# A second DMA transpose in place of seven TensorE transposes, with GpSimd taking two heads of a subtraction

## The chip, the cores and the metric

The kernel runs on one core of a Trainium2 chip. The metric is device time in microseconds (us). A core has five engines that run their own instruction queues side by side and wait for each other by semaphores: TensorE (PE in the profile; weight loads are listed apart as PEld), VectorE (DVE), ScalarE (ACT), GpSimd (POOL) and SyncE (SP), which here only issues transfers. Transfers run on 16 DMA engines that all queues share.

## The reference

Linear attention, followed by a two-layer network without biases:

```
q_s = exp(q - max(q, axis=-1));  q_s = q_s / sum(q_s, axis=-1)      # softmax over the 64 features
k_s = exp(k - max(k, axis=2));   k_s = k_s / sum(k_s, axis=2)       # softmax over the 576 positions
kv  = einsum('bhsd,bhse->bhde', k_s, v)                             # 64 x 64 for each batch and head
att = einsum('bhsd,bhde->bhse', q_s, kv)
x   = att transposed to (batch * position, head * feature)          # 4608 x 512
out = maximum(0.01 * h, h) @ w_out   with  h = x @ w_in             # 512 -> 2048 -> 512
```

q, k and v are 8 batches x 8 heads x 576 positions x 64 features of float32; the output is 4608 x 512 float32.

## The kernel before

**Two jobs, one instruction stream.** The network works on nine tiles of 512 tokens (`t` from 0 to 8). For a tile, `layer1` (L548, its matmul is L550) makes 16 blocks of 128 x 512 in PSUM, ScalarE puts each through the leaky ReLU into `gj` (L559), and `layer2` (L570, matmul L571) sums them into the output; then the result is copied to `out_sb` (L565) and stored (L568). The attention of the batches 1 to 7 is woven into these tiles. The call `at(t, u, f, ...)` hangs pieces of work on a place, and `run(t, u)` emits them there: u from 0 to 15 is after layer 1's block u, u from 16 to 31 is within layer 2. Tile 0 is cut finer: u from 0 to 31 are the blocks of its two halves and 32 to 47 are the 16 steps of layer 2 (so `at(0, 44, ...)` comes after its thirteenth step). The schedule is written out by hand: on each engine, instructions stand in the order in which the code emits them, and an instruction that waits holds up all that is behind it on its engine.

**Layout.** A batch's q, k or v is 128 partitions x 4 heads of the partition's half x 9 rows x 64 features (`HL`, `R`, `D`; one partition half holds four of the eight heads, the other half the other four). "Heads 0, 1" (`H0`) and "heads 2, 3" (`H1`) are the halves of the `HL` axis, and `gg` 0 and 1 are the same halves in the cross products. `R7` is rows 0 to 6, `RE` rows 7 and 8.

**k of a batch.** `k_tree` takes the maximum over the nine rows by four `tensor_tensor` steps (L153), `k_allmax` (L155) takes it over the partitions into `kall`, `k_sub` subtracts it in place (L186), `k_exp` makes `ke` (L194, ScalarE). `v_cast` makes the bfloat16 v with a column of ones (L204 on ScalarE, L206 on GpSimd). `kv` multiplies `ke` and v on TensorE (L328); `kd_make` divides by the sum (L348, L349).

**q of a batch.** `q_max` (L229), `q_sub` (L291), `q_exp` (L299), `q_sum` with the reciprocal (L308, L310), `q_norm` (L315). Then q has to be turned, so that features lie on partitions. Either TensorE does it against an identity matrix, and the result is copied from PSUM (`q_turn_first` L268 with `q_keep_first` L281, L282, L284, L286; `q_transpose` L432 with `q_keep` L447), or SP issues a DMA transpose (`q_turn` L538, `turn_next` L544). `cross` (L464) multiplies the turned q by `kd`.

**Batch 1** is special. Its rows 0 to 6 are wanted in tile 1, together with batch 0's last row: `attend_next` (L525) makes these cross products near the end of tile 0, heads 0, 1 first and then heads 2, 3, and copies them to `xT` (L533). Before the change, heads 0, 1 are turned by a DMA transpose of seven blocks into the tile `X1`, issued by `next_loads` ahead of four loads, and heads 2, 3 by seven TensorE transposes into `qT`, copied from PSUM half by ScalarE and half by VectorE. Rows 7 and 8 go by a later DMA transpose of four blocks into the end of `X1`. The exponential of heads 0, 1 stands before that of heads 2, 3 everywhere.

**Queues around the change.** SP's queue holds, in order: batch 1's k and q, `more_loads` (batch 1's v in two halves, batch 2's first k half), `next_loads`, the stores of tile 0, the loads of batch 3. GpSimd's holds the loads of the weights (L126, L131), then batch 1's `q_sub` of heads 0, 1, the `k_sub` of head 0, the `q_sub` of heads 2, 3.

Of the kernel before, what the change touches and what calls it, by code (L numbers as in the profile page):

```python
# [25 lines left out]
def kernel(  # L26
# [48 lines left out]
    def load(src, b, name, cuts, t=None):  # L75
        t = raw(name) if t is None else t
        flat = src[b].rearrange("h s d -> (h s d)").rearrange(
            "(hl p r d) -> p hl r d", hl=HL, p=P, r=R
        )
        for hs, rs in cuts:  # L80
            nc.sync.dma_start(  # L81
                out=t[:, hs, rs].rearrange("p h r d -> p h (r d)"),
                in_=flat[:, hs, rs].rearrange("p h r d -> p h (r d)"),
            )
        return t
# [133 lines left out]
    def q_begin(b):  # L219
        st[b]["qe"] = qe_pool.tile([P, R, HL, D], BF16, name="qe")  # L220
        if b == 1:
            st[b]["X1"] = const_pool.tile([P, R7.stop + 2 * (R - R7.stop), P], BF16, name="X1")
        if b < 2:
            st[b]["qT"] = qT_pool.tile([P, NB, R, L], BF16, name="qT", tag="qT")

    def q_max(b, rs, hs=ALLH):
# [50 lines left out]

    def q_keep_first(eng, b, gg, rs=RA):
        o, i = st[b]["qT"][:, gg::2, rs], st[b]["ps2", gg]
        if type(eng) is tuple:  # L280
            eng[0].copy(out=o[:, 0], in_=i[:, 0])  # L281
            eng[1].tensor_copy(out=o[:, 1], in_=i[:, 1])  # L282
        elif eng is nc.scalar:
            eng.copy(out=o, in_=i)  # L284
        else:
            eng.tensor_copy(out=o, in_=i)  # L286
# [164 lines left out]
    def cross(b, gg, outs, rows):  # L451
        for hp in range(2):
            for hh in range(2):
                half = slice(hp * D, (hp + 1) * D)
                ls = slice(hh * L, (hh + 1) * L)
                if b == 1 and rows.start == R7.stop:
                    rhs = st[b]["X1"][:, R7.stop :].rearrange("c (r g) l -> c g r l", g=2)[:, gg, :, ls]
                elif b == 1 and gg == 0:
                    rhs = st[b]["X1"][:, rows, ls]
                elif "qX" in st[b]:  # L460
                    rhs = st[b]["qX"].rearrange("c (r g) (h l) -> c g h r l", g=2, h=2)[:, gg, hh, rows]
                else:
                    rhs = st[b]["qT"][:, 2 * hh + gg, rows]
                nc.tensor.matmul(  # L464
                    outs[hp][hh * D : (hh + 1) * D].rearrange("p (r l) -> p r l", l=L),
                    lhsT=kd0[half, gg, hh, hp] if b == 0 else kd2[b % 2][half, gg, hh],
                    rhs=rhs[half],
                    start=True,
                    stop=True,
                )  # L470
# [72 lines left out]
    def turn_next(cols, blocks):  # L543
        nc.sync.dma_start_transpose(  # L544
            out=st[1]["X1"][:, blocks], in_=st[1]["qe"].rearrange("p r h d -> p (r h d)")[:, cols]
        )
# [35 lines left out]
    def at(t, u, *fns):  # L582
        while t > 0 and u >= 32:
            t, u = t + 1, u - 32
        hooks.setdefault((t, u), []).extend(fns)
# [87 lines left out]
    def more_loads():  # L673
        st[1]["v"] = t = raw("v_raw")
        nc.scalar.copy(out=t[0:1, 0, 0, 0:1], in_=identf[0:1, 0:1])
        load(v, 1, "v_raw", [(H0, ALLR), (H1, ALLR)], t)
        st[2]["k"] = load(k, 2, "k_raw", [(H0, ALLR)])

    def next_loads():
        turn_next(slice(0, 7 * 2 * D), slice(0, 7))  # L680
        load(q, 1, "q_raw", [(ALLH, RE)], st[1]["q"])
        load(k, 2, "k_raw", [(H1, ALLR)], st[2]["k"])
        st[2]["q"] = load(q, 2, "q_raw", [(ALLH, ALLR)])
        st[2]["v"] = load(v, 2, "v_raw", [(ALLH, ALLR)])
# [1 line left out]

    at(0, 20, lambda: k_begin(1), lambda: q_begin(1), lambda: k_tree(1, H0), lambda: k_tree(1, H1))
    at(0, 20, lambda: q_max(1, R7, H0), lambda: q_sub(nc.gpsimd, 1, R7, H0), lambda: k_allmax(1))
    at(0, 20, lambda: k_sub(nc.vector, 1, H1), lambda: k_sub(nc.gpsimd, 1, slice(0, 1)))
    at(0, 20, lambda: k_sub(nc.vector, 1, slice(1, 2)))  # L690
    at(0, 20, lambda: q_max(1, R7, H1), lambda: q_sub(nc.gpsimd, 1, R7, H1))
    at(0, 27, more_loads)
    at(0, 31, lambda: q_exp(1, R7, H0), lambda: q_sum(1, R7, H0), lambda: q_norm(1, R7, H0))
    at(0, 31, lambda: k_exp(1, H1), lambda: k_exp(1, H0), lambda: v_cast(nc.scalar, 1, 0))
    at(0, 32, lambda: q_exp(1, R7, H1), lambda: q_sum(1, R7, H1), lambda: q_norm(1, R7, H1))
    at(0, 32, next_loads)
    at(0, 32, lambda: v_cast(nc.scalar, 1, 1))
    at(0, 44, lambda: kv(1), lambda: kd_make(1))
    at(0, 45, lambda: q_turn_first(1, 1, R7), lambda: q_keep_first((nc.scalar, nc.vector), 1, 1, R7))
    at(0, 45, lambda: q_transpose(0, 8, 1), lambda: q_keep(nc.scalar, 0, 8, 1))  # L700
    at(0, 45, lambda: k_begin(2), lambda: q_begin(2), lambda: k_tree(2, H0, slice(0, 1)))
    at(0, 46, attend_next)
    at(1, 0, lambda: q_max(1, RE), lambda: q_sub(nc.gpsimd, 1, RE))
    at(1, 5, lambda: q_exp(1, RE))
# [3 lines left out]

    def plan2():
        b = 2  # L710
        at(1, 0, lambda: k_tree(b, H0, slice(1, 4)), lambda: k_tree(b, H1))
        at(1, 3, lambda: q_max(b, XR[0]), lambda: q_sub(nc.gpsimd, b, XR[0]))
        at(1, 3, lambda: k_allmax(b), lambda: k_sub(nc.vector, b, H0), lambda: k_sub(nc.vector, b, H1))
        at(1, 6, lambda: q_max(b, XR[1]), lambda: q_sub(nc.gpsimd, b, XR[1]))
        at(1, 11, lambda: q_exp(b, XR[0]), lambda: q_sum(b, XR[0]), lambda: q_norm(b, XR[0]))
        at(1, 13, lambda: v_cast(nc.gpsimd, b, 0), lambda: v_cast(nc.gpsimd, b, 1))
        at(1, 14, lambda: q_sum(1, RE), lambda: q_norm(1, RE))
        at(1, 15, lambda: k_exp(b, ALLH), lambda: q_turn(b, XR[0]))
        at(1, 15, lambda: turn_next(slice(7 * HL * D, R * HL * D), slice(7, 11)))
        at(1, 16, lambda: q_exp(b, XR[1]), lambda: q_sum(b, XR[1]), lambda: q_norm(b, XR[1]))  # L720
        at(1, 17, lambda: q_turn(b, XR[1]))
        at(1, 17, lambda: load_all(4))
        at(1, 23, lambda: kv(b))
        at(1, 24, lambda: kd_make(b))
        at(1, 27, lambda: attend_all(b, (XR[0],)), lambda: attend_all(1, (RE,)))

    plan2()

    def k_front(b, t, u, v):
        at(t, u, lambda: k_begin(b), lambda: q_begin(b), lambda: k_tree(b, ALLH))  # L730
        at(t, v, lambda: k_allmax(b), lambda: k_sub(nc.vector, b, ALLH))

    def q_front(b, t, u):
        at(t, u, lambda: q_max(b, ALLR), lambda: q_sub(nc.vector, b, ALLR))
# [8 lines left out]
    q_front(3, 1, 28)  # L743
    casts(3, 2, 0)
    at(2, 2, lambda: k_exp(3, ALLH))
    k_front(4, 2, 7, 17)
    at(2, 8, lambda: q_exp(3, ALLR))
    q_back(3, 2, 9)
    at(2, 9, lambda: load_all(5))
    casts(4, 2, 12)  # L750
    at(2, 19, lambda: kv(3, lambda: attend_all(2, (XR[1],))), lambda: kd_make(3))
    at(2, 22, lambda: k_exp(4, ALLH))
    at(2, 27, lambda: attend_kv(3))
    for t in range(3, B - 1):
        b = t + 1
# [150 lines left out]
```

## Time and profile before

| what | value |
|---|---|
| median of the runs | 282.12 us (lowest 282.04) |
| the profiled execution, whole | 282.16 us |
| its span, first to last instruction | 280.4 us |
| TensorE busy | 271.9 us, 1936 matmuls |
| VectorE, ScalarE, GpSimd busy | 161.8, 159.9, 48.6 us |
| mean granted clock of TensorE | 1.000 |
| SP's load of batch 2's first k half issued | 31.2 us |
| the DMA transpose of batch 1's heads 0, 1 issued | 40.3 us |
| layer 1 of tile 1 begins | 46.9 us |

All times inside the execution are counted from the span's start. The profile is of one execution, and differs a little from the median; sums are made against its own time. A row of a timeline gives start, duration, engine, line, operation, output and inputs with their shapes (partitions x elements), and in brackets the idle time ahead of it with what ended it. A group's row in the list of lines gives shapes, count, busy time and mean. "x7" after a row means seven instructions merged into one.

### The profile page before, as it was taken

The page shows a single profiled execution, that of the slowest core. Times are in us where ns is not written, and L with a number is a line of the kernel's source. Part 1 is how long each engine was busy: PE and PEld are TensorE (multiplying, and loading weights), DVE is VectorE, ACT ScalarE, POOL GpSimd, SP SyncE. Part 2 cuts the span into 40 slices and gives each one's busy share as a digit, 9 for nine tenths or more (in the row PEclk, how much of TensorE's full clock was granted, in tenths as well). Part 3 has the DMA queues.
Part 4 walks back from the last instruction along what each step waited for, and adds up shares of the span by engine and source line. Part 5 has one row for each costly group of instructions (what it writes and reads, how often), then busy time and mean ns, then how long its engine had stood idle before and what let it go on. Part 6 is the DMA issues. An engine that isn't in the chain of part 4 may idle for free.

```text
span 280.4 us, 4869 instructions
## 1 busy us (share of the span) xinstructions
PE 271.9 (97%) x1936; PEld 133.4 (48%) x1963; DVE 161.8 (58%) x228; ACT 159.9 (57%) x283; POOL 48.6 (17%) x54
## 2 busy tenths in 40 slices
PE   8799999999999999999999999999999999999994
PEld 3478645444444544444444444454444444444443
DVE  3986897999999959956794588543700000000021
ACT  4976673783488177754676448744844364146400
POOL 2947530258003003000500050000000000000000
PEclk9999999999999999999999999999999999999999
DMA  7999999897692598099309930333033300330033
GB/s 247 334 210 328 239 301 319 327 360 221 200 393 93 90 351 303 1 265 400 80 0 294 367 81 2 84 77 75 1 87 75 71 4 2 75 75 2 0 75 75
DMA packets 38678, 46.15 MB, mean 165 GB/s; under 512 B 17536, under 2 KB 21888, under 8 KB 38656
## 3 DMA queue, kind: packets, MB, share of 16 engines
q1 hardware_dynamic: 35136, 41.53, 47.0%
q0 software_dynamic: 3360, 4.20, 8.5%
q8 instruction: 15, 0.25, 0.3%
q10 hardware_dynamic: 160, 0.13, 0.2%
q14 instruction: 7, 0.06, 0.1%
HBM read 36.70 MB, written 9.44 MB: 165 GB/s over the span
## 4 chain that ended last, share of the span: by engine, by line
PE 90%; DMA 5%; POOL 2%; issue 1%; SPq 0%; ACT 0%; DVE 0%; ACTq 0%
PE pout L571 44%; PE ph L550 42%; DMA w_in_sb<-in_moe_w_in_dram 3%; DMA k_raw<-in_k_dram 2%; PE po L464 1%; PE pokv L328 1%; POOL w_in_sb L126 1%; PE pkv L328 1%; POOL vb L206 0%; POOL qe L257 0%; SPq L81 0%; ACT gj L559 0%; PE psum_q L268 0%; PE pokv L464 0%; DVE out_sb L565 0%
## 5 line engine op out<-in xcount | busy, mean ns | idle before, releaser
L571 PE MATMUL pout<-w_out_sb,gj 128*128 128x512 bf16 (+2 forms) x574 | 126.3, 373 | 1.0 <-issue 0.2
L550 PE MATMUL ph<-xT,w_in_sb 128*128 128x512 bf16 (+1 forms) x631 | 126.2, 357 | 0.7 <-DMA w_in_sb<-in_moe_w_in_dram 0.3
L559 ACT ACTIVATE gj<-ph 128x512 bf16<-128x512 f32 x144 | 82.0, 602 | 25.8 <-PE ph L550 25.0
L550 PEld LDWEIGHTS <-w_in_sb 128*128 128x128 bf16 x640 | 62.4, 98 | 62.4 <-DMA w_in_sb<-in_moe_w_in_dram 0.5
L571 PEld LDWEIGHTS <-gj 128*128 128x128 bf16 x592 | 56.5, 98 | 65.2 <-issue 0.2
L565 ACT COPY out_sb<-pout 128x512 f32<-128x512 f32 (+1 forms) x29 | 16.7, 580 | 66.9 <-PE pout L571 43.3
L565 DVE COPY out_sb<-pout 128x512 f32<-128x512 f32 (+1 forms) x8 | 4.8, 636 | 70.8 <-PE pout L571 70.8
L206 POOL CAST vb<-v_raw 128x1152 bf16<-128x1152 f32 x13 | 21.4, 1671 | 82.7 <-DMA v_raw<-in_v_dram 82.7
L308 DVE TENSOR_REDUCE qsum<-qe 128x36 f32<-128x2304 bf16 (+5 forms) x13 | 20.0, 1542 | 10.2 <-ACT qe L299 10.1
L194 ACT ACTIVATE ke<-k_raw 128x2304 bf16<-128x2304 f32 (+2 forms) x11 | 17.6, 1599 | 10.9 <-DVE k_raw L186 10.8
L315 DVE TENSOR_TENSOR qe<-qe,qrec 128x2304 bf16<-128x2304 bf16 (+5 forms) x13 | 22.0, 1689 | 0.4
L229 DVE TENSOR_REDUCE qmax<-q_raw 128x36 f32<-128x2304 f32 (+5 forms) x13 | 20.0, 1538 | 0.4 <-DMA q_raw<-in_q_dram 0.4
L186 DVE TENSOR_TENSOR k_raw<-k_raw,kall 128x2304 f32<-128x2304 f32 (+2 forms) x9 | 19.1, 2143 | 0.4
L299 ACT ACTIVATE qe<-q_raw 128x2304 bf16<-128x2304 f32 (+5 forms) x13 | 17.1, 1317 | 3.8 <-POOL q_raw L291 2.8
L153 DVE TENSOR_TENSOR t<-t 128x256 f32<-128x256 f32 (+2 forms) x22 | 15.5, 706 | 0.7
L487 ACT CAST xT<-po 128x512 bf16<-128x512 f32 (+3 forms) x34 | 15.3, 540 | 1.1 <-PE po L464 1.1
L291 POOL TENSOR_TENSOR q_raw<-q_raw,qmax 128x512 f32<-128x512 f32 (+3 forms) x7 | 10.8, 1547 | 21.9 <-DVE qmax L229 20.7
L291 DVE TENSOR_TENSOR q_raw<-q_raw,qmax 128x2304 f32<-128x2304 f32 (+1 forms) x6 | 13.2, 2202 | 0.3
L348 DVE RECIPROCAL krec<-pokv 128x2 f32<-128x2 f32 x8 | 1.3, 165 | 20.6 <-PE pokv L464 20.6
L153 DVE TENSOR_TENSOR t<-k_raw 128x512 f32<-128x512 f32 (+1 forms) x11 | 12.1, 1102 | 0.9 <-DMA k_raw<-in_k_dram 0.7
L360 PE MATMUL pout<-zero 128*128 128x512 f32 (+3 forms) x18 | 8.4, 587 | 1.0 <-POOL zero L100 1.0
L328 PEld LDWEIGHTS <-ke 64*64 64x64 bf16 x504 | 5.9, 107 | 3.6 <-issue 2.5
(70 smaller groups left out, 106.2 us busy)
## 6 DMA issues: line engine op xcount, KB each, us to landing
out_dram<-out_sb SPq DMA_DIRECT2D x70, 128.0 KB, 2.6
q_raw<-in_q_dram SPq DMA_DIRECT2D x6, 1152.0 KB, 8.5
v_raw<-in_v_dram SPq DMA_DIRECT2D x6, 1152.0 KB, 11.5
k_raw<-in_k_dram SPq DMA_DIRECT2D x5, 1152.0 KB, 6.4
k_raw<-in_k_dram SPq DMA_DIRECT2D x6, 576.0 KB, 5.7
v_raw<-in_v_dram SPq DMA_DIRECT2D x4, 576.0 KB, 7.5
w_in_sb<-in_moe_w_in_dram POOLq DMA_DIRECT2D x8, 256.0 KB, 6.9
w_out_sb<-in_moe_w_out_dram POOLq DMA_DIRECT2D x6, 256.0 KB, 9.3
```

What stands on the lines that cost most here:

```text
L153: nc.vector.tensor_tensor(out=o, in0=i0, in1=i1, op=ALU.max)
L186: eng.tensor_tensor(out=ks, in0=ks, in1=st[b]["kall"][:, hs].unsqueeze(2).to_broadcast([P, n, R, D]), op=ALU.subtract,)
L194: nc.scalar.activation(out=st[b]["ke"][:, :, hs].rearrange("p r h d -> p h r d"), in_=st[b]["k"][:, hs], func=AF.Exp,)
L206: eng.tensor_copy(out=o, in_=i)
L229: nc.vector.tensor_reduce(out=o, in_=st[b]["q"][:, hs, rs], axis=AX.X, op=ALU.max)
L291: eng.tensor_tensor(out=qs, in0=qs, in1=st[b]["qmax", rs.start, hs.start].unsqueeze(3).to_broadcast([P, m, n, D]), op=ALU.subtract,)
L308: nc.vector.reduce_sum(out=qsum, in_=q_cols(b, rs, hs), axis=AX.X)
L315: nc.vector.tensor_tensor(out=qes, in0=qes, in1=st[b]["qrec", rs.start, hs.start].unsqueeze(3).to_broadcast([P, n, m, D]), op=ALU.mult,)
L550: nc.tensor.matmul(ph, lhsT=w_in_sb[:, cb, j * P : (j + 1) * P], rhs=xT[:, cb, c0 : c0 + n], start=(cb == 0 and first), stop=(cb == NB - 1 ...
L559: nc.scalar.activation(out=o, in_=ph, func=AF.Prelu, alpha=LEAKY_SLOPE)
L565: copy(out=out_sb, in_=pout)
L571: nc.tensor.matmul(pout, lhsT=g_sb[j // 2][:, j % 2, tsub * P : (tsub + 1) * P], rhs=w_out_sb[:, j, os], start=(j == 0), stop=(j == NF - 1),)
```

## The change

Five things are edited; the lines are those of the kernel before.

- Batch 1's rows 0 to 6 of heads 2, 3 are turned by a second `turn_next` of seven blocks, right behind the first one in `next_loads`. The seven TensorE transposes and the two PSUM copies go, with the branch of `q_keep_first` that served them. `X1` grows from 11 to 18 blocks, and batch 1 needs no `qT`.
- GpSimd subtracts k's heads 0 and 1 (1152 columns) in one instruction, where it did head 0 (576 columns) and VectorE did head 1.
- ScalarE casts both halves of v after the exponential of q's heads 2, 3; one of the two stood before it.
- The load of batch 2's k, heads 0, 1, is issued behind the two transposes instead of behind batch 1's v. The first step of its `k_tree` and the claiming of its tiles move from tile 0's end to tile 1's first place. The exponential of batch 2's q rows 0 to 5 comes one place later.
- Batch 4's `k_sub` (VectorE) and `k_exp` (ScalarE) are each made in two halves of the heads.

```diff
     def q_begin(b):
         st[b]["qe"] = qe_pool.tile([P, R, HL, D], BF16, name="qe")
         if b == 1:
-            st[b]["X1"] = const_pool.tile([P, R7.stop + 2 * (R - R7.stop), P], BF16, name="X1")
-        if b < 2:
+            st[b]["X1"] = const_pool.tile([P, 2 * R, P], BF16, name="X1")
+        if b == 0:
             st[b]["qT"] = qT_pool.tile([P, NB, R, L], BF16, name="qT", tag="qT")
...
                 if b == 1 and rows.start == R7.stop:
-                    rhs = st[b]["X1"][:, R7.stop :].rearrange("c (r g) l -> c g r l", g=2)[:, gg, :, ls]
-                elif b == 1 and gg == 0:
-                    rhs = st[b]["X1"][:, rows, ls]
+                    rhs = st[b]["X1"][:, 2 * R7.stop :].rearrange("c (r g) l -> c g r l", g=2)[:, gg, :, ls]
+                elif b == 1:
+                    rhs = st[b]["X1"][:, gg * R7.stop : (gg + 1) * R7.stop, ls]
...
         load(v, 1, "v_raw", [(H0, ALLR), (H1, ALLR)], t)
-        st[2]["k"] = load(k, 2, "k_raw", [(H0, ALLR)])
 
     def next_loads():
         turn_next(slice(0, 7 * 2 * D), slice(0, 7))
+        turn_next(slice(7 * 2 * D, 14 * 2 * D), slice(7, 14))
+        st[2]["k"] = load(k, 2, "k_raw", [(H0, ALLR)])
         load(q, 1, "q_raw", [(ALLH, RE)], st[1]["q"])
...
-    at(0, 20, lambda: k_sub(nc.vector, 1, H1), lambda: k_sub(nc.gpsimd, 1, slice(0, 1)))
-    at(0, 20, lambda: k_sub(nc.vector, 1, slice(1, 2)))
+    at(0, 20, lambda: k_sub(nc.vector, 1, H1), lambda: k_sub(nc.gpsimd, 1, H0))
...
-    at(0, 31, lambda: k_exp(1, H1), lambda: k_exp(1, H0), lambda: v_cast(nc.scalar, 1, 0))
+    at(0, 31, lambda: k_exp(1, H1), lambda: k_exp(1, H0))
     at(0, 32, lambda: q_exp(1, R7, H1), lambda: q_sum(1, R7, H1), lambda: q_norm(1, R7, H1))
     at(0, 32, next_loads)
-    at(0, 32, lambda: v_cast(nc.scalar, 1, 1))
+    at(0, 32, lambda: v_cast(nc.scalar, 1, 0), lambda: v_cast(nc.scalar, 1, 1))
     at(0, 44, lambda: kv(1), lambda: kd_make(1))
-    at(0, 45, lambda: q_turn_first(1, 1, R7), lambda: q_keep_first((nc.scalar, nc.vector), 1, 1, R7))
-    at(0, 45, lambda: q_transpose(0, 8, 1), lambda: q_keep(nc.scalar, 0, 8, 1))
-    at(0, 45, lambda: k_begin(2), lambda: q_begin(2), lambda: k_tree(2, H0, slice(0, 1)))
+    at(0, 44, lambda: q_transpose(0, 8, 1), lambda: q_keep(nc.scalar, 0, 8, 1))
...
-        at(1, 0, lambda: k_tree(b, H0, slice(1, 4)), lambda: k_tree(b, H1))
+        at(1, 0, lambda: k_begin(b), lambda: q_begin(b), lambda: k_tree(b, H0), lambda: k_tree(b, H1))
...
-        at(1, 11, lambda: q_exp(b, XR[0]), lambda: q_sum(b, XR[0]), lambda: q_norm(b, XR[0]))
+        at(1, 12, lambda: q_exp(b, XR[0]), lambda: q_sum(b, XR[0]), lambda: q_norm(b, XR[0]))
...
-    def k_front(b, t, u, v):
+    def k_front(b, t, u, v, parts=(ALLH,)):
         at(t, u, lambda: k_begin(b), lambda: q_begin(b), lambda: k_tree(b, ALLH))
-        at(t, v, lambda: k_allmax(b), lambda: k_sub(nc.vector, b, ALLH))
+        at(t, v, lambda: k_allmax(b), *[lambda hs=hs: k_sub(nc.vector, b, hs) for hs in parts])
...
-    k_front(4, 2, 7, 17)
+    k_front(4, 2, 7, 17, (H0, H1))
...
-    at(2, 22, lambda: k_exp(4, ALLH))
+    at(2, 22, lambda: k_exp(4, H0), lambda: k_exp(4, H1))
```

More of the change, by code (lines that the diff above doesn't have):

```diff
@@ L279, in q_keep_first @@
         o, i = st[b]["qT"][:, gg::2, rs], st[b]["ps2", gg]
[L280 to L283, printed above, removed]
+        if eng is nc.scalar:
             eng.copy(out=o, in_=i)
@@ L718, in plan2 @@
         at(1, 15, lambda: k_exp(b, ALLH), lambda: q_turn(b, XR[0]))
-        at(1, 15, lambda: turn_next(slice(7 * HL * D, R * HL * D), slice(7, 11)))
+        at(1, 15, lambda: turn_next(slice(7 * HL * D, R * HL * D), slice(14, 18)))
         at(1, 16, lambda: q_exp(b, XR[1]), lambda: q_sum(b, XR[1]), lambda: q_norm(b, XR[1]))
```

## The prediction

> **What bounds the kernel.** I read the page's busy shares first, then the chain that ended last, then the waits of TensorE.
>
> ```profile
> PE 271.9 (97%) x1936; PEld 133.4 (48%) x1963; DVE 161.8 (58%) x228; ACT 159.9 (57%) x283; POOL 48.6 (17%) x54
> ...
> PE 90%; DMA 5%; POOL 2%; issue 1%; SPq 0%; ACT 0%; DVE 0%; ACTq 0%
> ```
>
> TensorE (PE) is busy for 97% of the span and makes 90% of the chain. Its granted clock is 9 or more tenths in every slice (mean 1.000). The waits of TensorE are 3.2 us in all, nearly all before 22.3 us. From there on a TensorE instruction that goes is time gained, and a wait put in front of TensorE is time lost, one for one. So I looked at the edited stretch in the chain in order of time (start, duration, what):
>
> ```profile
> 42.37 0.80 PE pkv L328 x72
> ...
> 44.15 0.39 PE psum_q L268 x7
> 44.54 0.11 PE psum_qt L432 x2
> 44.65 0.86 PE pout L571 x4
> 45.51 0.57 PE po L464 x16
> 46.08 0.97 PE pout L571 x4
> ```
>
> The reader is to see that no gap lies between these pieces: the seven transposes of L268 stand on the path with 0.39 us.
>
> **Step 1: the transposes leave TensorE.** Seven of 56 ns each: **-0.39 us**. Nothing else waits there, so the next work simply moves up. Their two PSUM copies go too (ScalarE 0.53 us, VectorE 0.39 us), both beside TensorE. On the profiled execution (282.16 us, 1.76 us of it around the span of 280.4) this is 281.77; against the median of 282.12, which is 0.04 lower, 281.73.
>
> **Step 2: the transfer that replaces them must land in time.** The cross products of batch 1's heads 2, 3 start at 45.72 now (the last four matmuls of L464); 0.39 earlier is **45.33**. That is the deadline. The new transfer can go only when VectorE has normalised those heads. The chain to it, from the timelines of the three engines (start, duration, engine, line):
>
> ```profile
> 34.55 1.97 DVE L186 TENSOR_TENSOR k_raw<-k_raw,kall 128x576 f32<-128x576 f32 x1
> 36.44 1.07 DVE L229 TENSOR_REDUCE qmax<-q_raw 128x14 f32<-128x896 f32 x1
> 37.44 1.07 DVE L308 TENSOR_REDUCE qsum<-qe 128x14 f32<-128x896 bf16 x1
> 38.54 0.24 DVE L310 RECIPROCAL qrec<-qsum 128x14 f32<-128x14 f32 x1
> 38.81 1.41 DVE L315 TENSOR_TENSOR qe<-qe,qrec 128x896 bf16<-128x896 bf16 x1
> 40.30 1.09 DVE L308 TENSOR_REDUCE qsum<-qe 128x14 f32<-128x896 bf16 x1
> 41.42 0.24 DVE L310 RECIPROCAL qrec<-qsum 128x14 f32<-128x14 f32 x1
> 41.69 1.09 DVE L315 TENSOR_TENSOR qe<-qe,qrec 128x896 bf16<-128x896 bf16 x1
> ```
> ```profile
> 33.32 2.58 POOL L186 TENSOR_TENSOR k_raw<-k_raw,kall 128x576 f32<-128x576 f32 x1 [0.49 <-DVE kall L178]
> 37.59 1.69 POOL L291 TENSOR_TENSOR q_raw<-q_raw,qmax 128x896 f32<-128x896 f32 x1 [1.70 <-DVE qmax L229]
> ```
> ```profile
> 36.60 1.16 ACT L194 ACTIVATE ke<-k_raw 128x1152 bf16<-128x1152 f32 x1 [0.77 <-DVE k_raw L186]
> 37.67 1.14 ACT L204 CAST vb<-v_raw 128x1152 bf16<-128x1152 f32 x1
> 39.31 0.95 ACT L299 ACTIVATE qe<-q_raw 128x896 bf16<-128x896 f32 x1 [0.51 <-POOL q_raw L291]
> 40.40 1.15 ACT L204 CAST vb<-v_raw 128x1152 bf16<-128x1152 f32 x1
> ```
>
> How long is GpSimd's subtraction of 1152 columns? Its own rows of this shape (L291) are 1.68 us for 896 columns and 2.76 for 1536, so 1.69 ns a column: 2.11 for 1152, 1.14 for 576. The 576 took 2.58, because VectorE's subtraction of 1152 columns ran from 33.27 to 34.63 beside it: 34.63 + 1.14 is 35.77, and it ended at 35.90. VectorE's 576 ended at 36.52, 0.62 after that; L397 does 576 in 0.70. So the two took turns, with 0.13 us at the handover. From below the new row costs 2.11 with no waiting (end 35.4); from above, twice the 2.58 (end 38.5). I take turns, since that row fits: 34.63 + 0.13 + 2.11 = **36.87**.
>
> VectorE loses the 576 columns, and its maximum of heads 2, 3 starts at 34.55 instead of 36.44: all up to the reciprocal moves up by 1.89, and the normalisation of heads 0, 1 is ready at 36.92. GpSimd's q subtraction of heads 2, 3 (the maximum is done at 35.6) starts at 36.87, just ahead, and ends at 38.55. The normalisation ends 0.94 after it, as now (40.22 against 39.28): 39.49, and the first transfer goes at 39.56 instead of 40.29. ScalarE: exponential of k's heads 0, 1 from 36.9 to 38.1; of q's heads 2, 3 from 38.58 to 39.53. VectorE: sum from 39.57, reciprocal 40.69, normalisation 40.96 to 42.05. The second transfer is issued at **42.12**.
>
> To landing, the seven blocks of the first transfer took 4.3 us, behind batch 2's first k load and other loads in the queue. Later transposes with nothing ahead: 2.4 (four blocks), 2.5 (six), 3.3 (twelve). The change takes that k load from ahead of both and puts it behind, so I take 2.6 from the near rows: landed at **44.7**, 0.6 us before the deadline. With 4.3 it is 46.4, a wait of 1.1. Cost taken: nothing; kept for the range: 0 to +1.1.
>
> **Step 3: v's casts behind q's exponential.** They run 39.5 to 40.6 and 40.6 to 41.7 (1.14 and 1.15); the products k*v begin at 42.37 (the second cast ends at 41.55 now). Nothing, with 0.7 us of cover.
>
> **Step 4: loads of batch 2.** SP issues k's heads 0, 1 at some 43.5 instead of 31.2, then q's last rows, k's heads 2, 3, q and v. By the issue-to-landing rows at that place (3.6 for q's rows, 4.9 for 576 KB of k, 8.3 for 1152 KB of q), plus 1.5 us for the 576 KB more that go ahead (at some 400 GB/s), k's first half is there by 48.5, q's rows by 49.5, k's second by 50.6, q by 55. VectorE takes them at 49.2, 49.9, 51.9 and 53.9: q could hold it for a microsecond by this generous sum; data alone (3.7 MB at 400 GB/s from 44.3) gives 52. SP's stores and batch 3's loads follow in the same order as before.
>
> **Step 5: the first maximum of batch 2's k** (0.68 us, now in a gap of VectorE at 45.45) goes into the stretch from 47.2 to 76 where VectorE has no gap. Layer 2's last copies start 0.45 earlier, so VectorE is about +0.25 late, and 0.64 against TensorE. The tightest place behind that is batch 4's k:
>
> ```profile
> 96.36 2.56 DVE L186 TENSOR_TENSOR k_raw<-k_raw,kall 128x2304 f32<-128x2304 f32 x1
> ...
> 98.95 2.12 ACT L194 ACTIVATE ke<-k_raw 128x2304 bf16<-128x2304 f32 x1 [4.03 <-DVE k_raw L186]
> ```
>
> It ends at 101.07, and TensorE reads it from 101.31. With 0.64 gone it would wait 0.4. In halves (1.35 and 1.16 each) ScalarE starts after the first: 96.6 + 2.70 + 1.16 is 100.5, before 100.9. Nothing, and it would cost 0.4 whole. Batch 2's casts on GpSimd end at 67.0 and move to 67.3; their products need them at 67.3 and 67.7 (by halves). Nothing. The exponential of batch 2's q behind one more activation stays before its sum (60.2 against 61.9).
>
> **The sum**: -0.39 and five times nothing: 281.73.
>
> **Weighed: one rule of the Trainium skill.** SBUF — State Buffer, section "Who interferes with whom", has it that a VectorE instruction with two SBUF inputs and a GpSimd instruction that reads SBUF block each other for a whole instruction, and that issue order decides who waits. The rows of step 2 agree (2.58 and 1.97 us where 1.14 and 0.70 are their own). By this rule the 0.05 us between GpSimd's q subtraction and VectorE's normalisation could as well fall the other way; that is rival A, worked out from rows.
>
> **Rivals.**
> A. *VectorE goes first at 36.92.* The normalisation then runs to 38.01, q's subtraction to 39.8, the exponential to 40.8, the sum from 40.83, the normalisation to 43.3; the second transfer goes at 43.38 and lands at 46.0. v's second cast ends at 42.9, 0.15 after its products want it. Wait in all 0.7, less 0.39: +0.3, **282.4**. For it: 0.05 us is less than these sums are good to. Against: GpSimd is ready first by them.
> B. *Slower: the second transfer is slow,* as the first was. It decides from a landing at 45.33 on, which is 3.2 us after the issue; at 4.3 the wait is 1.1 and the time +0.7, **282.8**. For it: the only row of this shape in this place. Against: its k load is no longer ahead. Equal in price: GpSimd's new row at twice 2.58, ending at 38.5.
> C. *The gain is not there,* because VectorE's lateness of 0.64 meets TensorE elsewhere (batch 2's casts, q's load): **282.1**. For it: 15 us of VectorE without a gap. Against: the nearest cover is 0.4.
> D. A and B together: landing at 47.7, +2, **284**.
>
> **How the numbers follow.** Forecast 0.55; A 0.2; B 0.12; C 0.08; D 0.05. The times shown of the kernel before (282.04, the median 282.12, the profiled 282.16) agree to 0.12; with as much as step 1's 0.39 being off, the forecast's own width is 281.3 to 282.1. For 8 in 10 the range takes in A and B: **281.3 to 283.0**. All of them lie within 2% (5.6 us), which is about what a measurement of this kernel can tell from no change: 0.97 within, 0.01 faster, 0.02 slower.
>
> **What would show it.** Step 1: no L268-like group at 44, TensorE's layer-1 row of the second tile group at 46.5 instead of 46.9. Step 2: GpSimd's 1152 columns with 3.5 us from 33.3, the second transfer issued at 42.1 and landed by 45; a TensorE wait on that transfer at 45.3 would show A or B, told apart by its issue (43.4) or its landing time (4.3). Step 5: the second half of batch 4's exponential ending by 100.6. The prediction is wrong if TensorE idles anywhere between 42 and 102.

## The result, and the profile after

The changed kernel takes 284.48 us by the median of six executions (283.9 to 286.05), the kernel before 282.13 beside it (five of its six lie at 281.98 to 282.28, one took 411.41): a ratio of 1.0092, 95% interval 1.0076 to 1.0108. That is 2.3 us slower, inside the 2% that the prediction called no change, and 1.5 us above the top of its range. The profiled execution took 283.9 us, the lowest of the six, with a span of 282.1. So the profiles account for 1.74 us; the other 0.6 of the median has no trace.

The groups and lines of the changed kernel stand three lower than before (the cross products are L461, the transfers into `X1` L541). First the waits of TensorE (line waited for, us in total, times, longest), then the chain in order of time (start, duration, what), both of the changed kernel:

```profile
PE po L461 <- DMA X<-qe: 1.5, 1, 1.5
```
```profile
42.54 0.75 PE pkv L325 x66
43.30 3.77 DMA X<-qe
...
47.12 0.38 PE po L461 x4
47.50 0.97 PE pout L568 x4
48.47 13.81 PE ph L547 x64
62.28 5.49 PE pout L568 x26
67.77 5.81 DMA qX<-qe
...
73.62 0.53 PE po L461 x8
...
74.16 0.31 PE po L461 x8
74.46 3.56 PE pout L568 x16
78.02 2.16 PE ph L547 x10
```

Two transfers stand in it now. Against the chain of the kernel before, the sum of the profiled executions is:

| stretch | before | after | difference |
|---|---|---|---|
| start to the products k*v of batch 1 | 42.37 | 42.54 | +0.17 |
| from there to the first cross product (45.51; after 45.29, where the layer 2 matmuls ahead of it end) | 3.14 | 2.75 | -0.39 |
| from there to layer 1 of tile 1 (47.05; 48.47) | 1.54 | 3.18 | +1.64 |
| from there to layer 1 of tile 2 (76.18; 78.02) | 29.13 | 29.55 | +0.42 |
| from there to the end of the span | 204.2 | 204.1 | -0.1 |

The seven transposes did bring their 0.39. The wait on the second transfer took 1.46 of the 1.64, and there is a second loss 26 us later, of 0.42, that no rival of the prediction had. How the second transfer came to be late, from the timelines of VectorE, GpSimd and SP of the changed kernel:

```profile
34.67 1.08 DVE L229 TENSOR_REDUCE qmax<-q_raw 128x14 f32<-128x896 f32 x1
37.05 1.14 DVE L312 TENSOR_TENSOR qe<-qe,qrec 128x896 bf16<-128x896 bf16 x1
40.74 1.09 DVE L305 TENSOR_REDUCE qsum<-qe 128x14 f32<-128x896 bf16 x1 [2.56 <-ACT qe L296]
42.14 1.09 DVE L312 TENSOR_TENSOR qe<-qe,qrec 128x896 bf16<-128x896 bf16 x1
```
```profile
33.44 3.80 POOL L186 TENSOR_TENSOR k_raw<-k_raw,kall 128x1152 f32<-128x1152 f32 x1 [0.49 <-DVE kall L178]
37.20 2.54 POOL L288 TENSOR_TENSOR q_raw<-q_raw,qmax 128x896 f32<-128x896 f32 x1
```
```profile
43.30 2.53 SPq L541 DMA_TRANSPOSE X<-qe  x1
45.92 0.54 SPq L81 DMA_DIRECT2D k_raw<-in_k_dram  x1
...
58.62 0.54 SPq L81 DMA_DIRECT2D k_raw<-in_k_dram  x1
...
67.77 2.18 SPq L535 DMA_TRANSPOSE qX<-qe  x1
```

Two rows of SP in the kernel before, to set against the last two:

```profile
54.77 0.54 SPq L81 DMA_DIRECT2D k_raw<-in_k_dram  x1
...
66.17 1.31 SPq L538 DMA_TRANSPOSE qX<-qe  x1
```

VectorE's normalisation began at 37.05, while GpSimd was still at its 1152 columns until 37.24. So VectorE went first; GpSimd's next subtraction took 2.54 us instead of the 1.69 it had alone, and the transfer was issued at 43.30 instead of 42.12. It landed 3.8 us later, at 47.1, and everything that SP had behind it followed later: batch 2's loads at 45.9 and batch 3's at 58.6 (54.8 before).

Why did it take 3.8 us? The next two fences are of the DMA view, in 40 equal slices: of the changed kernel from 42.9 to 46.9, GB/s in each slice and then the instruction queue's packets and MB; and of a kernel of the experiments (`e6` below) with its second transfer issued at 43.8, GB/s from 43.4 to 47.0.

```profile
GB/s 0 0 0 0 0 0 0 0 0 0 0 164 0 0 0 18 166 259 271 269 248 56 3 0 5 8 8 3 10 15 10 10 49 276 289 282 39 0 0 0
...
q8 instruction: 1, 0.02, 2.1%
```
```profile
GB/s 89 6 0 0 0 0 0 0 0 0 0 0 0 0 0 0 0 0 119 265 282 290 293 287 290 293 276 140 14 0 0 0 26 102 128 51 26 51 0 51
```

In the second kernel the transposition is one piece of 0.9 us. In the changed kernel it is two, with a microsecond of hardly any traffic between them, and one packet of the instruction queue (16 KB of program, the slice with 164 GB/s) lies ahead of the gap. By the packet's own times it ran from 44.04 to 45.37. No view here tells which DMA engine a packet ran on, so by what route it holds the transposition up is not shown; that it does is tested below.

In this document a granted clock is given where it counts: some executions of kernels with such a wait show 0.993 to 0.994 instead of 1.0 and are some 1.5 to 2.4 us longer (286.05 is the only one of the changed kernel's six).

### The profile page after: what moved, and what is told of

Its sections match the earlier page's. It is cut to its first block, busy times and chain, and to the rows that moved or that the text cites. A ratio compares the mean times of both kernels' runs of the same rounds, so it can differ in the third digit from the quotient of the medians.

```text
span 282.1 us, 4883 instructions
## 1 busy us (share of the span) xinstructions
PE 273.7 (97%) x1956; PEld 133.1 (47%) x1956; DVE 160.4 (57%) x227; ACT 159.7 (57%) x283; POOL 51.3 (18%) x54
## 4 chain that ended last, share of the span: by engine, by line
PE 87%; DMA 9%; POOL 2%; SPq 0%; issue 0%; DVE 0%
PE ph L547 42%; PE pout L568 42%; DMA w_in_sb<-in_moe_w_in_dram 3%; DMA qX<-qe 2%; DMA k_raw<-in_k_dram 2%; DMA X<-qe 1%; PE po L461 1%; POOL w_in_sb L126 1%; PE pokv L325 1%; PE pkv L325 1%; POOL vb L206 0%; SPq L81 0%; POOL qe L257 0%; PE pokv L461 0%; DVE out_sb L562 0%
## 5 line engine op out<-in xcount | busy, mean ns | idle before, releaser
L568 PE MATMUL pout<-w_out_sb,gj 128*128 128x512 bf16 (+2 forms) x592 | 127.6, 373 | 0.0
L194 ACT ACTIVATE ke<-k_raw 128x1152 bf16<-128x1152 f32 (+2 forms) x12 | 17.8, 1483 | 11.4 <-DVE k_raw L186 9.9
L312 DVE TENSOR_TENSOR qe<-qe,qrec 128x2304 bf16<-128x2304 bf16 (+5 forms) x13 | 20.7, 1592 | 0.4
L186 DVE TENSOR_TENSOR k_raw<-k_raw,kall 128x1152 f32<-128x1152 f32 (+1 forms) x9 | 17.3, 1942 | 0.4
L288 POOL TENSOR_TENSOR q_raw<-q_raw,qmax 128x512 f32<-128x512 f32 (+3 forms) x7 | 11.9, 1706 | 21.1 <-DVE qmax L229 20.0
L153 DVE TENSOR_TENSOR t<-k_raw 128x512 f32<-128x512 f32 (+1 forms) x11 | 13.1, 1191 | 1.0 <-DMA k_raw<-in_k_dram 0.9
```

Of the source, the lines that this page charges most:

```text
L153: nc.vector.tensor_tensor(out=o, in0=i0, in1=i1, op=ALU.max)
L186: eng.tensor_tensor(out=ks, in0=ks, in1=st[b]["kall"][:, hs].unsqueeze(2).to_broadcast([P, n, R, D]), op=ALU.subtract,)
L194: nc.scalar.activation(out=st[b]["ke"][:, :, hs].rearrange("p r h d -> p h r d"), in_=st[b]["k"][:, hs], func=AF.Exp,)
L288: eng.tensor_tensor(out=qs, in0=qs, in1=st[b]["qmax", rs.start, hs.start].unsqueeze(3).to_broadcast([P, m, n, D]), op=ALU.subtract,)
L312: nc.vector.tensor_tensor(out=qes, in0=qes, in1=st[b]["qrec", rs.start, hs.start].unsqueeze(3).to_broadcast([P, n, m, D]), op=ALU.mult,)
L568: nc.tensor.matmul(pout, lhsT=g_sb[j // 2][:, j % 2, tsub * P : (tsub + 1) * P], rhs=w_out_sb[:, j, os], start=(j == 0), stop=(j == NF - 1),)
```

## The experiments

The theory from these traces has three causes: the flipped order of VectorE and GpSimd (later issue), the instruction transfer (slow landing), and the loads that stand behind the second transfer in SP's queue (the second loss). The rival is that the other edits, or lateness of VectorE, cost the time. All times are medians; the kernel before beside each set was at 282.01 to 282.29.

**The other edits alone** (`e1_turn_on_tensor`): the changed kernel with heads 2, 3 turned by TensorE as before.

```diff
-        turn_next(slice(7 * 2 * D, 14 * 2 * D), slice(7, 14))
...
+    at(0, 45, lambda: q_turn_first(1, 1, R7), lambda: q_keep_first((nc.scalar, nc.vector), 1, 1, R7))
```

> The changed kernel with heads 2, 3 of batch 1 turned by TensorE again and copied from PSUM, all other edits kept. Theory T (the loss comes only from the second transfer: TensorE waits for it, and SP holds five loads behind it): 281.9 to 282.4 us, no TensorE wait on a transfer after 23 us, batch 2's loads issued from about 39.7. Rival O (the other edits cost by themselves: GpSimd's 1152 columns, batch 2's first k half loaded later, 0.68 us more for VectorE in tile 1): 283 us or more.

282.5 us, ratio 1.0011 (1.0002 to 1.002). VectorE goes first here too (GpSimd's subtraction takes 2.54 from 37.40), batch 3's first load is issued at 54.4 and no transfer holds TensorE. So the other edits cost some 0.3 us (0.1 to 0.6 by the interval) and the transfer nearly all the rest. In its traced execution all that they cost lies ahead of layer 1 of tile 1; part of it is the cover of the v casts, which the flipped order used up (timeline of TensorE of this kernel):

```profile
43.07 0.48 PE L328 MATMUL pkv<-vb,ke 64*64 64x65 bf16 x36 [0.16 <-ACT vb L204]
```

**The transfer alone** (`e2_transfer_alone`): the kernel before, with only the second transfer in place of the transposes.

```diff
         turn_next(slice(0, 7 * 2 * D), slice(0, 7))
+        turn_next(slice(7 * 2 * D, 14 * 2 * D), slice(7, 14))
...
-    at(0, 45, lambda: q_turn_first(1, 1, R7), lambda: q_keep_first((nc.scalar, nc.vector), 1, 1, R7))
```

> The kernel before with the second transfer as its only edit: GpSimd keeps 576 columns, batch 2's first k half is still loaded ahead. The order of GpSimd and VectorE is then that of before, and the transfer is issued at about 42.9 (normalisation ends at 42.8). Theory T: it lands at 45.5 (2.6 us) to 46.7 (3.8 us), TensorE waits 0.2 to 1.4, the loads behind it are 2.5 us late: 282.3 to 284.0 us. Rival G (without VectorE going ahead of GpSimd nothing is late): 281.7 to 282.0 us.

283.41 us, ratio 1.0041 (1.0027 to 1.0055). Here both transfers are waited for (timeline of TensorE of this kernel):

```profile
46.26 0.38 PE L464 MATMUL po<-X,kd 64*64 64x448 bf16 x4 [1.13 <-DMA X<-qe]
...
47.04 0.38 PE L464 MATMUL po<-X,kd 64*64 64x448 bf16 x4 [0.36 <-DMA X<-qe]
```

The first was issued at 40.19 and landed in 6.0, behind batch 2's k load; the second at 42.7, landing in 4.2, with the 16 KB packet at 43.76 beside it. The replacement loses by itself; the edits that come with it make the first transfer early and the second no earlier. Batch 3's first load went at 58.0 here and at 54.4 in `e1`: what makes those loads late is the transfer standing ahead of batch 2's loads in SP's queue, and not the k load that was moved.

**Loads between the two transfers** (`e3_loads_between`): the changed kernel, the second transfer moved behind batch 2's first k half and q's last rows.

```diff
         turn_next(slice(0, 7 * 2 * D), slice(0, 7))
-        turn_next(slice(7 * 2 * D, 14 * 2 * D), slice(7, 14))
         st[2]["k"] = load(k, 2, "k_raw", [(H0, ALLR)])
         load(q, 1, "q_raw", [(ALLH, RE)], st[1]["q"])
+        turn_next(slice(7 * 2 * D, 14 * 2 * D), slice(7, 14))
```

> The changed kernel with batch 2's first k half and batch 1's last q rows (832 KB) loaded between the two transposes, so that SP issues them while the second one is not ready. Theory Q (part of the loss comes from loads that SP holds behind the second transpose; batch 3's loads then lie in front of batch 2's transposes): batch 2's loads end 2 us earlier, the wait at batch 2's cross products (73.6 in the changed kernel) goes, the second transpose lands no later than 47.1: 283.0 to 283.8 us. Rival: the 832 KB (2 us at 400 GB/s from 41 on) hold the second transpose up: lands at 48 or later, 285 us or more.

284.8 us, ratio 1.0092 (1.0064 to 1.012): three executions at 283.8 to 284.1 with a clock of 1.0, three at 285.5 to 286.3 with 0.993 to 0.994. By its trace the loads left from 40.2 on, while the second transfer was not ready until 43.80; it landed in 3.9 and was waited for 1.62. Batch 3's loads went at 56.8, and the second loss is gone: batch 2's first transpose landed in 3.4.

**GpSimd first** (`e4_gpsimd_first`): the changed kernel, with two more reciprocals (0.5 us) ahead of VectorE's normalisation of heads 0, 1.

```diff
-        nc.vector.reciprocal(out=qrec, in_=qsum)
+        for _ in range(times):
+            nc.vector.reciprocal(out=qrec, in_=qsum)
...
-    at(0, 31, lambda: q_exp(1, R7, H0), lambda: q_sum(1, R7, H0), lambda: q_norm(1, R7, H0))
+    at(0, 31, lambda: q_exp(1, R7, H0), lambda: q_sum(1, R7, H0, 3), lambda: q_norm(1, R7, H0))
```

> The changed kernel with the reciprocal of heads 0, 1 made three times, so that VectorE's normalisation asks 0.54 us later and GpSimd's q subtraction of heads 2, 3 goes first. Theory L (the order of these two sets the issue of the second transpose): GpSimd's subtraction 1.7 us long from 37.2, second transpose issued at 42.3 instead of 43.3, lands at 44.9 (2.6 us) to 46.1 (3.8 us): 282.3 to 283.6 us. Rival: the issue doesn't move, or the landing doesn't follow it: 284.3 to 284.7 us.

283.5 us, ratio 1.0068 (1.0039 to 1.0096). Of nine executions six have a clock of 0.997 or more (282.89 to 284.87, middle 283.25), three 0.993 to 0.994 (285.6). The order did turn (timelines of GpSimd and TensorE of this kernel):

```profile
37.92 1.70 POOL L288 TENSOR_TENSOR q_raw<-q_raw,qmax 128x896 f32<-128x896 f32 x1
```
```profile
47.01 0.38 PE L462 MATMUL po<-X,kd 64*64 64x448 bf16 x4 [1.47 <-DMA X<-qe]
```

In this execution the subtraction of k began 0.73 later than in the profile of the changed kernel (34.17), so the transfer left at 43.2 all the same; measured from that subtraction's start it left 0.84 sooner. It still landed in 3.8, with the 16 KB packet at 43.98, and was waited for 1.47, as in the changed kernel (1.46). Like against like (clock of 0.997 and up), the middle is 283.25 against 284.46. But of the 0.5 us between the two traced executions 0.4 is the second loss, which is gone here, and the wait did not move. So what the order is worth by itself is not shown.

**The instruction transfer moved** (`e5_pad_after`, `e6_pad_gpsimd_first`, `e7_pad_transfer_alone`, and the control `e8_pad_before`): 85 matmuls of 16 columns in place of three of the warm-up matmuls ahead of 13 us. With more instructions ahead, the 16 KB packets come at other times: at 44.0 and 67.9 us in the changed kernel, at 40.5, 51.9 and 72.5 with the edit (`e5`). The same edit went into the changed kernel, into GpSimd first, into the transfer alone and into the kernel before.

```diff
-    wake(TT, TT, TT, 256)
+    wake(TT, TT)
+    pad(60)
...
-    wake(384)
+    pad(25)
```

> The changed kernel with 85 small matmuls (64 x 64 weights, 16 columns) in place of three warm-up matmuls before 13 us, so that the 16 KB instruction transfer that ran from 44.0 to 45.4 comes some 160 TensorE instructions earlier in the program. Theory F (that transfer holds one of the 16 DMA engines for 1.3 us, and the second transpose, which needs all of them, waits): no such transfer between 43.3 and 46, the second transpose lands 2.6 to 2.9 us after its issue instead of 3.8, TensorE's wait falls from 1.5 to 0.3-0.6: 283.2 to 283.7 us. Rival S (3.8 us is what this transpose takes as the second of two): landing unchanged, 284.2 to 284.8 us.

> Both at once: the small matmuls, and the reciprocal of heads 0, 1 made three times so that GpSimd goes first. Theories L and F together: second transpose issued at 42.4 to 43.2 (later if the k data comes later, as it did by 0.7 us in the run with the reciprocal alone), landed 2.7 us later, 45.1 to 45.9, against a deadline of 45.3: TensorE waits 0 to 0.6, 281.7 to 282.6 us. Rival S: landed at 46.2 or later, 283 us or more.

> The kernel before with the second transpose as its only other edit, and the small matmuls. Theory F: the first transpose lands at 44.6 as in the kernel before (46.2 without the small matmuls), the second, issued at 42.8, at 45.4 to 45.8; TensorE waits 0.1 to 0.5 instead of 1.5: 281.9 to 282.5 us. Rival S: 283.2 to 283.6 us as without the small matmuls.

> The kernel before with the small matmuls alone: what they cost by themselves. All theories: nothing, 282.0 to 282.5 us; if they delay the first stage, TensorE's first layer-1 matmul behind the w_in wait (22.3) moves by as much as the time.

The control is 283.6 us itself (1.0041, 1.002 to 1.0061): with three warm-ups gone the granted clock is 0.66 from 13 to 17 us in its profile (0.50 from 9 to 17 in that of `e6`; `e5` kept 1.00). So these medians (284.41, 284.13 and 283.73) stand against 283.6, not against the kernel before, and of the time they say little. The traces say what they were made for: no instruction packet starts at 42 to 46 us in any of the three, and the second transfer lands in 2.6 us in each, issued at 44.0, 43.8 and 44.2. In the four kernels so far without this edit where a packet starts at 43.8 to 45.1 it took 3.8 to 4.2. In `e7` neither transfer is waited for (timeline of TensorE of this kernel; no row names a wait):

```profile
44.19 0.80 PE L328 MATMUL pkv<-vb,ke 64*64 64x65 bf16 x72
...
47.15 0.36 PE L464 MATMUL po<-X,kd 64*64 64x448 bf16 x4
...
48.31 1.03 PE L550 MATMUL ph<-xT,w_in_sb 128*128 128x512 bf16 x4
```

From the products k*v to layer 1 of tile 1 this is 4.12 us, against 4.51 in the kernel before (42.37 to 46.88) and in `e8`: here the transfer does gain the 0.39 that was forecast. In `e2`, the same kernel with the packet in its old place, it was 6.0. The margin was also some 0.5 us wider than in `e2`: TensorE came 2.0 later to this stretch, and the transfer left 1.5 later. The waits of TensorE in `e5`, which kept the clock and should have gained most:

```profile
PE po L461 <- DMA qX<-qe: 1.4, 1, 1.4
...
PE pkv L325 <- ACT vb L204: 0.7, 2, 0.6
...
PE po L461 <- DMA X<-qe: 0.3, 1, 0.3
```

The wait on the second transfer is down to 0.3, though it was issued at 44.0; the wait for the v casts ahead of it (0.7, pushed back by the flipped order) is part of that, since TensorE comes later. And batch 2's transpose is waited for 1.4: issued at 68.3, it landed in 6.4. The loads of batch 3 had left at 59.8, the latest of all kernels.

**Two causes away at once** (`e9_first_and_loads`): GpSimd first and the loads between, both edits as above.

> Two of the three causes are taken away at once: GpSimd's q subtraction is let go ahead of VectorE's normalisation (two extra reciprocals, 0.5 us on VectorE), and the two loads of 832 KB in all go between the two transfers again. Theory (three causes, which add: the flipped order, the slow landing, the late loads): the second transfer is issued at some 42.8 and lands 3.8 us later, at 46.6; the wait on it is 1.2 to 1.4; batch 2's first transpose lands 3.4 us after its issue and its cross products wait for nothing. Sum: -0.39, +0.25 (what the other edits cost with the transposes on TensorE), +1.3: 283.2, between 282.8 and 283.6 where the granted clock stays at 1.0. Rival (the causes do not add, the loads ahead of the transfer make it late by themselves): 284 or more, as with the loads between alone.

287.31 us, ratio 1.0189 (1.0173 to 1.0204), four times of four with a clock of 0.993 to 0.994. The theory's 283.2 was wrong by 4 us, and the rival was right that the causes do not add. The chain and the windows of this kernel (window, its length, busy us of PE, PEld, DVE, ACT, POOL with their counts, granted clock, DMA share, GB/s):

```profile
42.74 0.45 PE pkv L326 x34
43.19 6.51 DMA X<-qe
```
```profile
40.00:46.00 6.00, 5.29 (x103) 2.68 (x104) 4.22 (x9) 3.52 (x5) 0.00 (x0) 1.00 0.75 167
46.00:50.00 4.00, 0.25 (x4) 0.11 (x3) 0.28 (x1) 0.13 (x1) 0.00 (x0) 0.98 1.26 206
50.00:54.00 4.00, 4.00 (x15) 1.46 (x12) 3.65 (x7) 0.94 (x2) 0.00 (x0) 0.59 1.03 408
```

With GpSimd first, VectorE's normalisation of heads 0, 1 waits for it (2.22 us from 38.33), the first transfer goes at 40.62 and not at 38.75, and the two loads (832 KB) follow at 42.06 and 42.64. The second transfer comes right behind them at 43.19 and lands in 6.5 us. In `e3` the same loads had left three microseconds ahead of it, and it landed in 3.9. An instruction packet lies beside it in both (46.24 here, 45.06 in `e3`), so the 2.6 us between them go with how much of the loads is still to come when the transfer is issued; no run has the loads without a packet. TensorE stands for 4.2 us and then runs at 0.59 of its clock over the next four, which is another 1.6 us lost.

**All three** (`e10_all_three`, control `e11_small_warm_before`): the kernel above and the kernel before, with 75 warm-ups of 24 columns in place of the first four.

```diff
-    wake(TT, TT, TT, 256)
+    wake(*[24] * 75)
```

> As the run before, and the third cause taken away too: 75 warm-up matmuls of 24 columns take the place of the four ahead of 6 us (1792 columns, as now 1800), so that the instruction transfer of 16 KB that has lain at 43.8 to 45.1 comes some 3 us earlier. Theory: the second transfer lands 2.6 us after an issue at 42.8, at 45.4; the wait is 0 to 0.3, and the time is 282.0 to 282.4, no more than 0.3 from the kernel before. Rival (the slow landing has another cause than the instruction transfer): landing 3.8, 283.2 as in the run before. If the small warm-ups cost clock, the control beside it shows how much.

> The control: the kernel before with the 75 small warm-up matmuls alone. Theory: 282.1 to 282.4, its granted clock 1.0. Rival (fewer columns at a time hold the clock less well): 283.5 and a clock of 0.98 to 0.99, as with the 85 small matmuls before.

314.58 us (ratio 1.1104, 1.1027 to 1.1182) and 309.01 us (1.0959, 1.0941 to 1.0977). The edit is a failure: the warm-ups are float32, and those of 24 columns hold TensorE for 32.2 us, where the four wide ones took 5.2 (timeline of TensorE of the control):

```profile
0.99 32.19 PE L360 MATMUL pout<-zero 128*128 128x24 f32 x150 [0.99 <-POOL zero L100]
```

The difference is the 27 us by which both kernels are late from there on. Between themselves they differ by 5.6 us, as `e9` and the kernel before do (5.3), and `e10` waits 3.5 us for the second transfer, again behind the two loads, and with an instruction packet beside it after all. It doesn't test the three causes together.

**The late loads alone** (`e12_v3_later`): the changed kernel, with batch 3's v loaded behind batch 2's second transpose instead of ahead of the first.

```diff
-    at(1, 2, lambda: load_all(3))
+    at(1, 2, lambda: load_all(3, "kq"))
...
-        at(1, 17, lambda: load_all(4))
+        at(1, 17, lambda: load_all(3, "v"), lambda: load_all(4))
```

> The changed kernel, and of batch 3's loads v's (1152 KB) is issued behind batch 2's first qX transpose and the last transpose of X, instead of ahead of them. Nothing else is touched; batch 3's v is read 15 us later. Theory (the late loads are a cause of their own): the first qX transpose, issued at some 67.8, lands 3.3 to 3.8 us later instead of 5.8, batch 2's cross products at 73.6 wait for nothing, and the second tile group's last layer 2 products follow 0.3 to 0.5 us earlier than in the changed kernel; the wait of 1.5 on the second transfer at 45.5 stays. 284.0 to 284.2 by the median, against 284.5 (283.5 against 283.9 in an execution whose granted clock stays at 1.0). Rival (the transpose is late for another reason, for instance its normalisation on VectorE): landing above 5, 284.4 to 284.6.

283.48 us (282.93 to 283.56), ratio 1.0046 (1.0033 to 1.006): 1.0 less than the changed kernel, where 0.3 to 0.5 was expected. Its chain:

```profile
42.38 0.74 PE pkv L325 x66
43.11 3.37 DMA X<-qe
...
46.53 0.38 PE po L461 x4
46.91 0.97 PE pout L568 x4
47.88 4.96 PE ph L547 x23
...
72.90 0.56 PE po L461 x16
73.46 3.56 PE pout L568 x16
77.02 0.65 PE ph L547 x3
```

From layer 1 of tile 1 to that of tile 2 it takes 29.14 us, as before the change (29.13; 29.55 in the changed kernel): that loss was the late loads, 0.41 of the 1.0. The traced executions differ by 1.0 as well. Another 0.43 there is the second transfer itself, which landed in 3.4 instead of 3.8, its instruction packet having taken 0.96 us instead of 1.33, and 0.16 lies ahead of the products k*v, in front of all that was edited. Whether that holds for the other executions stays open.

The second loss can be followed over the kernels: when batch 3's first load was issued, when batch 2's first transpose was, where the 16 KB packet nearest to that transpose started, how long the transpose took to land, and the time from layer 1 of tile 1 to layer 1 of tile 2 (all in us; `e9` lost clock in that stretch).

| kernel | first load of batch 3 | transpose issued | packet | landing | tile 1 to tile 2 |
|---|---|---|---|---|---|
| before | 54.8 | 66.2 | 65.5 | 3.3 | 29.13 |
| `e1` | 54.4 | 67.2 | 65.4 | 3.3 | 29.13 |
| `e8` | 54.8 | 66.8 | 69.6 | 5.0 | 29.13 |
| `e3` | 56.8 | 68.4 | 68.2 | 3.4 | 29.14 |
| `e9` | 57.4 | 70.5 | 69.8 | 3.3 | - |
| `e4` | 57.9 | 67.6 | 67.4 | 5.0 | 29.14 |
| `e7` | 57.9 | 67.4 | 70.6 | 5.8 | 29.38 |
| `e2` | 58.0 | 66.9 | 68.2 | 5.2 | 29.13 |
| changed | 58.6 | 67.8 | 67.9 | 5.8 | 29.55 |
| `e6` | 59.8 | 68.9 | 72.2 | 5.4 | 29.55 |
| `e5` | 59.8 | 68.3 | 72.5 | 6.4 | 30.99 |
| `e12` (no v among the loads) | 58.4 | 67.2 | 67.9 | 4.3 | 29.14 |

Late loads are not the only thing that lengthens this landing. In `e8` the loads left as in the kernel before, a packet ran in the middle of the transposition, and it took 5.0. In `e12` the packet lies as in the changed kernel, and taking v's load away brings 5.8 down to 4.3; so the loads are at least 1.5 of the 2.5 by which the changed kernel's landing is longer than that of the kernel before. How the rest divides is not shown. A landing of up to 5.2 cost TensorE nothing.

Why batch 3's loads are four microseconds late: batch 2's v was issued at 48.12 instead of 43.41, and the first store of tile 0, which SP issues next, at 48.89 instead of 47.95, so that the stores now come right behind 3.7 MB of loads. Between 44 and 60 us SP's waits among the stores name batch 2's q and v loads for 4.9 us (2.3 and 2.6) and the output's copies for 0.8, where in the kernel before it was 1.8 for v and 4.6 for the copies. To landing the stores took (minimum, median, maximum; tile `out_sb` from 44 to 60 us), in the kernel before and in the changed one:

```profile
DMA to landing us min/median/max: 2.8/5.3/6.6
```
```profile
DMA to landing us min/median/max: 2.7/8.5/9.5
```

The last of the eight was issued at 58.06 instead of 54.21, with batch 3's loads behind it.

## Why the prediction was wrong, point by point

**Step 1 was right.** TensorE's stretch up to the first cross product is 0.39 shorter, as forecast, and in `e7`, where the transfer was in time, the whole stretch up to layer 1 of tile 1 is.

**Step 2 failed**, in two of its terms, and both the way its rivals had it. The end of GpSimd's 1152 columns was put at 36.87, by turns with a handover of 0.13. They ended at 37.24: 2.49 us after VectorE's subtraction (34.75) and not 2.24. The two took turns, as the step had it, and the size was off by 0.25 us (2.49 less the 2.11 reckoned for the subtraction alone leaves 0.38 for the handover, not 0.13); but the step had decided an order by 0.05 us. So VectorE went first, which is rival A; its issue of 43.38 was 43.30. The rule of the Trainium skill that the prediction weighed (SBUF — State Buffer, section "Who interferes with whom": the two block each other for a whole instruction, and issue order decides who waits) holds in these rows, 2.54 us for a subtraction that takes 1.69 when GpSimd is first. The other term, and the one that the experiments bear out, is the landing of 2.6: that is what it takes when neither a packet nor loads lie beside it (`e5`, `e6`, `e7`), and the changed kernel's took 3.8. The step gave the k load as its reason for the 2.6, and the k load decided neither transfer: the first one took 4.9 in the changed kernel with that load out of the way, issued 2.0 us earlier (4.3 before), and the second took 2.6 in `e7` with it in place. The step asked only for loads ahead of the transfer, and not for the 16 KB of instructions, which rival B's 4.3 did not have as its reason either. The measured 3.8 lies between the two.

**Rival D is what happened**, A and B together: 284 forecast, 284.48 measured, the second loss among it. It was given 0.05 because A and B had 0.2 and 0.12, and both were too low: the reason against A (GpSimd is ready first "by these sums") was a margin smaller than the error of the sums, and the one against B named a load that was not the cause. That the number comes so near is in part luck: D had the landing at 47.7 and with it a wait of 2.4, measured were 47.1 and 1.46, and the second loss, which D did not have, made up for some of it.

**Step 3's cover of 0.7 was gone** with the order: the second half of the products waited for the casts 0.16 us in `e1`, 0.32 in `e3`, 0.57 in `e5`, as rival A's 0.15 said; in the changed kernel's profile they do not wait.

**Step 4 failed in its last sentence.** That SP's stores and batch 3's loads follow in the same order was right, and that this costs nothing was wrong. Batch 2's own loads were in time (no wait of TensorE names them), but through the stores the delay came to batch 3's loads, and these lay ahead of the transposes of tile 1's end, whose landing TensorE waits for. In the changed kernel's profile it comes 0.14 late to the products that read batch 2's first transpose, and those that read batch 1's rows 7 and 8 come another 0.28 late: that transpose, next in the queue, landed in 4.1 instead of 2.4. That is the 0.42; in `e5` the wait is 1.4. The step looked at who takes batch 2's loads, and not at which transfer with a deadline comes behind them when the second transfer holds them up.

**Step 5 was right in its result.** The halves of batch 4's exponential ended at 102.71, 0.44 us ahead of the products that read them (103.15). In `e1`, without the stall, at 101.01 against 101.70. That is 0.4 later than the 100.6 forecast, and still ahead of TensorE; no run has these edits with batch 4's exponential whole, so what the halves saved is not shown.

**Rival C did not happen.** From layer 1 of tile 1 to that of tile 2 `e1` takes 29.13 us, as the kernel before, though it has all of VectorE's lateness; its 0.4 by the profile lies ahead of layer 1 of tile 1 (47.45 against 47.05), 0.16 of it the wait for the v cast.

The statement that a wait ahead of TensorE is time lost one for one was too low for some of them: after the 4.2 us of `e9` the clock fell as well, and shorter waits sometimes go with a lower clock (below).

## What to carry to other kernels

A transfer that replaces work on the bounding engine has a deadline, and its landing time is a property of what else is on the DMA engines, loads queued ahead of it and instruction fetches included: sum its chain with the slowest landing that the traces show, and call it free only if that is in time. A transfer moved ahead of loads in a queue delays all that stands behind; follow the queue on to the next transfer that has a deadline. And where two instructions on VectorE and GpSimd become ready within a few tenths of each other, both orders belong in the sum with equal weight.

## What the runs showed that was not expected

- Where a 16 KB packet of the instruction queue ran during the second transposition of seven blocks, it landed in 3.4 to 4.2 us (the changed kernel, `e2`, `e3`, `e4`, `e12`); with none beside it, in 2.6 (`e5`, `e6`, `e7`). One of twelve blocks took 5.0 with a packet in its middle (`e8`) and 3.3 without (the kernel before). Such a packet took 0.9 to 1.7 us. Where it falls moved with the number of instructions ahead of it, so an edit that has nothing to do with a transfer can put one beside it.
- A transfer of the same size right behind two loads of 832 KB in all, with a packet beside it too, took 6.5 us (`e9`).
- A wait of 1.5 us on TensorE sometimes goes with a lower clock: an execution with 0.993 to 0.994 came in one of six of the changed kernel, three of six of `e3`, three of nine of `e4`; after the 4.2 us of `e9` in four of four. 0.006 of 282 us is 1.7 us, about what these executions lose. None of the 48 executions of the kernel before beside the experiments was below 0.997. But `e2`, with waits of 1.13 and 0.36, had none in five, and that the wait is the cause is not shown for these short ones.
